# One found order for every instruction of a delta-rule and mixture-of-experts kernel

## The chip, the cores and the metric

The kernel runs on one core of one Trainium2 chip. Its time is the device time of one launch in microseconds (us).

## The reference, cut to what matters

Three stages, float32 throughout. An attention layer keeps a 48x48 state for each of 32 heads and updates it token by token over 768 tokens (the delta rule). Its output, 3072 rows of 384, is routed: each row goes to one of 8 experts, a two-layer network of its own. The result goes through a last network with three first matrices, of whose outputs the largest is taken.

```python
for t in range(S):                                  # S = 768, for 4 x 8 heads, D = 48
    y[:, :, t] = einsum('bhd,bhde->bhe', q[:, :, t], state)
    v_old = einsum('bhde,bhd->bhe', state, k_n[:, :, t])
    state = state + beta[t] * einsum('bhd,bhe->bhde', k_n[:, :, t], v[:, :, t] - v_old)
logits = x @ w_gate + modality_bias[modality_id]    # x: 3072 x 384; 8 experts
e_idx = argmax(logits); gate_w = softmax(logits)[e_idx]
out[e_idx == e] = gate_w * (relu(x @ w1[e]) @ w2[e])   # 384 -> 1024 -> 384, for each e
h = maximum(maximum(x2 @ m1, x2 @ m2), x2 @ m3)        # 384 -> 768
return h @ m_out                                       # 768 -> 384
```

## The kernel before, in words

**Attention.** The 768 tokens are cut into 12 chunks C of 64; two chunks make a group g of 128. Every matrix is split into a high and a low 16-bit half, and a product is three matmuls (`mm3`, L145 to L147). For a group, `k_load`, `k_norm` and `k_split` load, scale and split the keys. For a chunk, `st_G` makes the products of the keys among themselves, and `g_out` and `at_load` carry them through DRAM into a layout in which `sub` inverts a triangular 32x32 system for all heads: 31 steps, each with a product (`stmp`, L508) and a difference (`W`, L510) on VectorE, and from step 10 on also on GpSimd. The inverse goes to DRAM (`Wd`) and back (`w_load` to tile `N`, then `w_split`). `st_Z`, `st_X`, `st_P` prepare the chunk; `st_R`, `st_U`, `st_S`, `st_O` are the recurrence. `st_S` of chunk C makes the state that chunk C+1 needs, `st_O` the output rows. "o" is the half of the heads; `st_S.4.0` is that step for chunk 4, half 0.

**Routing.** `route0` and `route1` of a chunk make logits, the expert of each row and its slot, and scatter the rows to the DRAM buffer `xs` (L745), where each expert has its own stretch. `select` picks the expert that has most rows waiting; after the last chunk `pad_zero` copies eight blocks of zero rows behind the experts' rows (L785).

**Experts.** `tiles` works through 12 tiles of 256 rows (one of 288). For a tile `tile_load` reads the expert's number and first row into registers (L800, L801) and loads the rows transposed (`mxT`, L804). The weights come in 8 parts f (`ws`, L817, L819, two buffers), are split on ScalarE and GpSimd (`wh` L827, `wl` L139), and used by `up` (`hp`, L838) and `down` (`accA`, `accB`, L867). The last network of the tile before (`second`: `pa`, `pb`, L888; `outp`: `po`, L905) goes between them. The step `more` advances this generator by half a part. `narrow_load` and `narrow` bring the last network's weights in and split them.

**What sets the order.** `STEPS` lists every step. Those ahead of a bar are given out as they stand, each engine runs them in that order. Those behind it carry a number after "@", which sets a priority, and a list scheduler orders the single instructions of all engines at build time by priority and by a timeline of its own. `side()` gives some instructions a higher priority there. What follows `STEPS` in `run` (the last tiles) goes through the same scheduler. Every engine then runs its own list in order, and so does each queue that issues loads and stores, SyncE's (SP) above all. The loop at the end of `run` runs over the rows that are left, here none.

Of the kernel before, what the change touches and what calls it, by code (L numbers as in the profile page):

```python
# [1 line left out]

# [6 lines left out]
F16 = mybir.dt.float16  # L9
# [10 lines left out]
WIDE = 288  # L20
RS = 3072 + WIDE
ZROW = 8 * RS
XROWS = ZROW + WIDE
XW = 784
MAGIC = 12582912.0
STEPS = """
# [89 lines left out]


AHEAD = 20000
class Kern:
    def __init__(self, tc, ctx, q, k, v, beta, mod_id, w_gate, mod_bias, w1, w2, m1, m2, m3, m_out, out):  # L120
        self.tc, self.nc, self.ctx = tc, tc.nc, ctx
# [5 lines left out]
        self.w1, self.w2, self.m, self.m_out, self.out = w1, w2, (m1, m2, m3), m_out, out  # L127
        self.S = q.shape[2]
        self.NG = self.S // 128
        self.NT = 4 * self.NG  # L130
        self.NC = 2 * self.NG

    def pool(self, ctx, name, bufs, **kw):
        return ctx.enter_context(self.tc.tile_pool(name=name, bufs=bufs, **kw))

    def lo(self, eng, out, in_, hi, scale=1.0):
        nc = self.nc
# [12 lines left out]
    def setup(self):  # L150
        nc, NG, ctx = self.nc, self.NG, self.ctx
        P = lambda n, b, **kw: self.pool(ctx, n, b, **kw)
        self.dr1 = P("dr1", 1, space=DRAM)
        self.dr = P("dr", 3, space=DRAM)
        self.c0 = P("c0", 1)
        self.tp = self.tile_pools(ctx, "a", 2, 3, False)
        self.sel = P("sel", 1)
        P = lambda n, b, **kw: self.pool(self.actx, n, b, **kw)
        self.psC = P("psC", 2, space=PSUM)
        self.psZ = P("psZ", 1, space=PSUM)  # L160
        c1 = self.c1 = P("c1", 1)
        self.ld = P("ld", 1)
        self.mg = P("mg", 1)
        self.ch = P("ch", 2)
        self.rt = P("rt", 1)
        self.xs = self.dr1.tile([XROWS, XW // 2], I32, name="xs")
# [535 lines left out]
    def route(self, C):  # L702
        nc, rt, x = self.nc, self.rt, [self.x[C, o] for o in range(2)]
# [14 lines left out]
        m2 = rt.tile([128, 2, 1], F32, name="m2")  # L718
# [23 lines left out]
        slot = rt.tile([128, 2], I32, name="slot")  # L742
        V.tensor_copy(slot, sl)
        for o in range(2):
            nc.gpsimd.indirect_dma_start(  # L745
                out=self.xs[:, :], out_offset=bass.IndirectOffsetOnAxis(ap=slot[:, o:o + 1], axis=0),
                in_=x[o][:, :], in_offset=None)
        yield

# [32 lines left out]
        return ri  # L782

    def pad_rows(self, r):
        self.nc.sync.dma_start(out=self.xs[bass.ds(r, WIDE), :], in_=self.xs[ZROW:XROWS, :])  # L785

    def pad_zero(self):
        nc, mx = self.nc, self.sel
# [7 lines left out]
    def tile_load(self, si, tp=None):  # L796
        nc = self.nc
        tp = tp or self.tp
        mx, w = tp["x"], tp["W"]
        e = nc.sync.value_load(si[0:1, 0:1], min_val=0, max_val=7)  # L800
        row = nc.sync.value_load(si[0:1, 1:2], min_val=0, max_val=ZROW)  # L801
        T = dict(e=e, w=w, tp=tp, ws={}, wb={}, cols=[(t, min(128, w - t)) for t in range(0, w, 128)])
        T["xT"] = mx.tile([128, 6, w], F16, name="mxT", bufs=3)
        nc.sync.dma_start_transpose(out=T["xT"], in_=self.xs[bass.ds(row, w), 0:384].bitcast(F16))  # L804
        T["ix"] = mx.tile([128, len(T["cols"]), 2], I32, name="ix", bufs=3)
        full = w // 128
        nc.sync.dma_start(out=T["ix"][:, 0:full], in_=self.xs[bass.ds(row, 128 * full), 384:386].rearrange("(t p) w -> p t w", p=128))
        if w > 128 * full:
            nc.sync.dma_start(out=T["ix"][0:w - 128 * full, full], in_=self.xs[bass.ds(row + 128 * full, w - 128 * full), 384:386])
        self.wt_load(T, 0)  # L810
        self.wt_load(T, 1)
        return T

    def wt_load(self, T, f):
        nc, e = self.nc, T["e"]
        ws = T["tp"]["w"].tile([128, 2, 384], F32, name="ws")
        nc.sync.dma_start(out=ws[:, 0].rearrange("p (k f) -> p k f", f=128),  # L817
                          in_=self.w1[bass.ds(e, 1), :, f * 128:(f + 1) * 128].rearrange("o (k p) f -> p (o k) f", p=128))
        nc.sync.dma_start(out=ws[:, 1], in_=self.w2[bass.ds(e, 1), f * 128:(f + 1) * 128, :].rearrange("o p d -> p (o d)"))  # L819
        T["ws"][f] = ws  # L820

    def wt_cast(self, T, f):
# [75 lines left out]
    def outp(self, T, t):  # L898
        nc, H = self.nc, T["H"]
        at, n = T["cols"][t]  # L900
        po = T["tp"]["psM"].tile([128, 384], F32, name="po", tag="m")
        i = 0
        for f in range(6):
            for a, b in (("h", "h"), ("h", "l"), ("l", "h")):
                nc.tensor.matmul(po[0:n], lhsT=H[a][:, f, at:at + n], rhs=self.mo[b][:, f], start=(i == 0), stop=(i == 17))  # L905
                i += 1
        ob = T["tp"]["x"].tile([128, 384], F32, name="ob", bufs=2)
        with self.side():
            nc.scalar.activation(ob[0:n], po[0:n], AF.Copy, scale=T["ix"].bitcast(F32)[0:n, t, 1:2])
        nc.gpsimd.indirect_dma_start(  # L910
            out=self.out[:, :], out_offset=bass.IndirectOffsetOnAxis(ap=T["ix"][0:n, t, 0:1], axis=0), in_=ob[0:n], in_offset=None,
            bounds_check=self.NT * 128 - 1, oob_is_err=False)

    def behind(self, T, f):
# [49 lines left out]
        next(self.moe)  # L964

    def side(self):
        return self.tc.high_priority(offset=AHEAD)

    def play(self, steps):
        tc = self.tc  # L970
        for step in steps.split():
            step, at = step.split("@")
            name, *args = step.split(".")
            tc.cur_priority = int(at) * 1000 + 1000000
            getattr(self, name)(*(int(a) if a.isdigit() else a for a in args))

    def run(self):
        nc, tc = self.nc, self.tc
        self.actx = ExitStack()
        self.setup()  # L980
        self.pieces, self.narrows, self.sis, self.moe = self.second_weights(), [], [], None
        E = mybir.EngineType
# [6 lines left out]
        self.sis.append((self.select(True),))  # L989
        for _ in self.moe:  # L990
            pass
        ri = self.remaining()
        regs = nc.values_load(ri[0:1, 0:1], min_val=0, max_val=18)
        with tc.For_i(0, regs, 1):
            for _ in self.tiles([(self.select(True),)]):
                pass
# [38 lines left out]
```

## Time and profile before

| | us |
|---|---|
| median of 3 runs | 973.54 |
| lowest, highest | 968.46, 976.4 |
| the profiled execution | 976.38 |
| its span, first to last instruction | 974.7 |

The profile is of one execution; 1.7 us of its time lie outside the span, and it is 2.8 us above the median. Times in the rows below count from the span's start. A row of the windows view gives, for a stretch, its length and then the busy time of each engine with the number of its instructions, TensorE's granted clock as a share of 2.4 GHz, and the share and rate of the DMA engines. In a row of a timeline or of the chain the first number is the start and the second the length.

### The profile page before, as it was taken

To read this page: it belongs to the slowest core of one execution; us is meant where nothing else is said; L and a number is where in the kernel's file an instruction comes from. 1 tells how busy PE (TensorE), PEld (TensorE's weight loads), DVE (VectorE), ACT (ScalarE), POOL (GpSimd) and SP (SyncE) were. 2 spreads that over 40 slices of the span, in tenths; PEclk is the share of its full clock that TensorE was granted. 3 is DMA by queue.
4 is the path that set the end of the run, shared out by engine and by line. 5 is a ranking of instruction groups with operands and counts; after the bars stand their busy time and mean duration, and the time that the engine had idled before them with its cause. 6 is when DMAs were issued, how large, how long until landed. Compare 5 with 4: busy or idle time off the path is not lost.

```text
span 974.7 us, 24604 instructions
## 1 busy us (share of the span) xinstructions
PE 701.5 (72%) x9442; PEld 580.6 (60%) x9442; DVE 646.8 (66%) x1552; ACT 434.8 (45%) x865; POOL 538.7 (55%) x694
## 2 busy tenths in 40 slices
PE   0324620487458877666788977899999997999994
PEld 0213520376337666565567756778788875887873
DVE  7688898688798499867998769757465441132220
ACT  2445542675344564434445534355364432344321
POOL 7173367556576677526767468664555443545421
PEclk9975855688568999879899989899999997999998
DMA  7796777786886737756688663456343345332200
GB/s 102 138 185 184 120 193 184 201 136 159 222 201 141 179 102 188 146 127 127 152 200 194 125 137 82 106 152 110 107 105 96 95 140 178 108 98 89 67 19 17
DMA packets 355322, 131.88 MB, mean 135 GB/s; under 512 B 290265, under 2 KB 346624, under 8 KB 355072
## 3 DMA queue, kind: packets, MB, share of 16 engines
q1 hardware_dynamic: 352096, 120.72, 54.5%
q0 software_dynamic: 3104, 9.54, 2.7%
q8 instruction: 76, 1.25, 0.5%
q14 instruction: 46, 0.38, 0.1%
HBM read 77.71 MB, written 34.10 MB: 115 GB/s over the span
## 4 chain that ended last, share of the span: by engine, by line
PE 29%; DVE 28%; DMA 7%; issue 6%; POOL 4%; ACT 3%; SPq 3%; POOLq 0%; DVEq 0%; ACTq 0%
PE pa L888 7%; DVE stmp L508 6%; PE hp L838 5%; DVE W L510 4%; PE pb L888 4%; PE po L905 4%; PE accA L867 3%; DMA xT<-xt 2%; PE accB L867 1%; DMA ws<-in_moe_w_dram 1%; DVE tl L581 1%; DMA xs<-xt,slot 1%; SPq L474 1%; POOL wl L139 1%; DVE hl L844 1%
## 5 line engine op out<-in xcount | busy, mean ns | idle before, releaser
L139 POOL TENSOR_TENSOR wl<-ws,wh 128x768 bf16<-128x768 f32 x96 | 159.2, 1659 | 71.3 <-ACT wh L827 69.4
L888 PE MATMUL pa<-x2T,mwh 128*128 128x256 f16 (+1 forms) x828 | 159.7, 284 | 14.7 <-DVE x2T L141 6.9
L838 PE MATMUL hp<-mxT,wh 128*128 128x256 f16 (+1 forms) x576 | 119.4, 283 | 49.1 <-ACT wh L827 42.3
L888 PEld LDWEIGHTS <-mwh 128*128 128x128 f16 x1296 | 129.8, 101 | 27.1 <-issue 7.6
L139 POOL TENSOR_TENSOR Hl<-mt,Hh 128x256 f16<-128x256 f32 (+1 forms) x72 | 49.8, 692 | 130.2 <-ACT Hh L895 127.9
L888 PE MATMUL pa<-x2T,mwl 128*128 128x256 f16 (+1 forms) x414 | 117.5, 284 | 0.0
L827 ACT ACTIVATE wh<-ws 128x768 f16<-128x768 f32 x96 | 80.5, 839 | 42.3 <-PE accB L867 21.5
L145 PEld LDWEIGHTS <-bkh 128*128 128x128 f16 x560 | 55.7, 106 | 59.8 <-DVE bkh L438 25.8
L508 DVE TENSOR_TENSOR stmp<-At,W 128x31 f32<-128x31 f32 (+29 forms) x155 | 88.2, 569 | 3.3 <-POOL At L497 0.4
L838 PEld LDWEIGHTS <-wh 128*128 128x128 f16 x576 | 57.7, 101 | 53.8 <-ACT wh L827 44.8
L888 PE MATMUL pb<-x2T,mwh 128*128 128x256 f16 (+1 forms) x432 | 86.7, 278 | 0.0
L844 DVE SCALAR_TENSOR_TENSOR hl<-hp,hh 128x256 f16<-128x256 f32 (+1 forms) x96 | 40.4, 421 | 66.5 <-ACT hh L843 62.9
L139 POOL TENSOR_TENSOR pl<-Pm,ph 64x512 f16<-64x512 f32 x48 | 57.0, 1188 | 47.6 <-ACT ph L634 39.1
L838 PE MATMUL hp<-mxT,wl 128*128 128x256 f16 (+1 forms) x288 | 81.4, 283 | 2.4 <-POOL wl L139 2.4
L895 ACT ACTIVATE Hh<-mt 128x256 f16<-128x256 f32 (+1 forms) x72 | 30.1, 418 | 104.6 <-DVE mt L894 104.5
L888 PEld LDWEIGHTS <-mwl 128*128 128x128 bf16 x648 | 65.1, 100 | 19.1 <-issue 9.5
L867 PEld LDWEIGHTS <-wh 128*128 128x128 f16 x576 | 57.6, 101 | 24.7 <-issue 15.6
L510 DVE TENSOR_TENSOR W<-W,stmp 128x31 f32<-128x31 f32 (+29 forms) x155 | 69.2, 447 | 3.0
L893 DVE TENSOR_TENSOR mt<-pa,mt 128x256 f32<-128x256 f32 x66 | 27.8, 421 | 61.1 <-ACT mt L892 57.5
L147 PEld LDWEIGHTS <-bkl 128*128 128x128 f16 x560 | 55.0, 106 | 8.3 <-issue 4.5
L888 PE MATMUL pb<-x2T,mwl 128*128 128x256 f16 (+1 forms) x216 | 59.9, 277 | 0.0
L867 PE MATMUL accA<-hh,wh 128*128 128x256 f16 (+1 forms) x184 | 52.0, 282 | 10.0 <-ACT hh L843 10.0
(286 smaller groups left out, 2583.6 us busy)
## 6 DMA issues: line engine op xcount, KB each, us to landing
ws<-in_moe_w_dram SPq DMA_DIRECT2D x192, 192.0 KB
nd<-in_moe_w_dram SPq DMA_DIRECT2D x18, 384.0 KB
vf<-in_v_dram SPq DMA_DIRECT2D x48, 96.0 KB
ring<-in_k_dram SPq DMA_DIRECT2D x10, 384.0 KB
ring<-in_q_dram SPq DMA_DIRECT2D x10, 384.0 KB
xs<-xs SPq DMA_DIRECT2D x8, 441.0 KB
N<-Wd SPq DMA_DIRECT2D x48, 64.0 KB
Qdh<-tmh SPq DMA_DIRECT2D x6, 512.0 KB
```

The costliest lines, as they stand in the source:

```text
L139: nc.gpsimd.tensor_tensor(out=out, in0=in_, in1=hi, op=ALU.subtract)
L145: mm(out, lhsT=ah, rhs=bh, start=start, stop=False)
L147: mm(out, lhsT=al, rhs=bh, start=False, stop=stop)
L508: E.tensor_tensor(out=tv, in0=At[:, j:j + 1, j + 1:].to_broadcast([128, m, n]), in1=W[:, r0:r1, j:j + 1].to_broadcast([128, m, n]), op=ALU ...
L510: E.tensor_tensor(out=W[:, r0:r1, j + 1:], in0=W[:, r0:r1, j + 1:], in1=tv, op=ALU.subtract)
L827: self.nc.scalar.activation(wh, ws, AF.Copy)
L838: nc.tensor.matmul(h, lhsT=a[:, 0, kk * 128:(kk + 1) * 128], rhs=xT[:, b], start=(n == 0), stop=(n == 8))
L844: nc.vector.scalar_tensor_tensor(out=hl, in0=h, scalar=0.0, in1=hh, op0=ALU.max, op1=ALU.subtract)
L867: nc.tensor.matmul(ps, lhsT=a[:, 1, ds], rhs=b, start=(f == 0 and i == 0 and d in first), stop=(f == 7 and i == 2 and d in last))
L888: nc.tensor.matmul(ps[i], lhsT=self.mw[a][:, i, kk, fs], rhs=x2T[:, b], start=(n == 0), stop=(n == 8))
L895: nc.scalar.activation(T["H"]["h"][:, f], mt, AF.Copy)
L905: nc.tensor.matmul(po[0:n], lhsT=H[a][:, f, at:at + n], rhs=self.mo[b][:, f], start=(i == 0), stop=(i == 17))
```

## The change

All calls that issue an instruction up to the last loop are recorded and not made. A `Book` stands in the place of `nc`: each call becomes an `Op`, and what it returns, a tile, a register or a pool, is a `Lazy` that is made when it is first asked for. Each instruction is a piece with a number of its own, in the order in which the source makes the calls; only matmuls that follow each other without a break share a piece, up to 32, or up to 9 in `more` and in the last tiles. `ORDER` is a list of all 4474 piece numbers. At the end the pieces are given out in that order, with no scheduler, for all five engines. The steps in `STEPS` and the instructions themselves stay as they were; the numbers after "@" and the bar are not used any more. Tiles take their buffers in the order of first use in `ORDER`. The loop behind stays as it was.

```diff
+ORDER = """
+2 6 3 0-1 180 5 23 13 179 181 8 63 12 14 178 148 19 9 4 21 7 66 11 22 83 105 10 84 20 17 15 18 106 16 150 29 146 85 80 149 77 43 86 55 74 81 31 36 70
...
+"""
+class Op(Lazy):
...
+    def get(self):
+        if not self.done:
+            self.done = True
+            self.val = self.fn(*real(self.args), **real(self.kw))
+        return self.val
...
+class Book:
...
+    def put(self, name, op):
+        if self.cut or name != "tensor" or self.pieces[-1][0] != name or len(self.pieces[-1][1]) == self.most:
+            self.pieces.append((name, []))
+            self.cut = False
+        self.pieces[-1][1].append(op)
...
+    def give(self, order):
+        assert sorted(order) == list(range(len(self.pieces))), (len(order), len(self.pieces))
+        for n in order:
+            for op in self.pieces[n][1]:
+                op.get()
+        self.open = False
...
     def side(self):
-        return self.tc.high_priority(offset=AHEAD)
+        return nullcontext() if self.nc.open else self.tc.high_priority(offset=AHEAD)
...
     def run(self):
-        nc, tc = self.nc, self.tc
+        tc, book = self.tc, self.nc
...
-        first, then = STEPS.split("|")
-        with tc.manual_schedule(engines={E.PE, E.DVE, E.Activation, E.Pool, E.SP}):
-            self.play(first)
-        self.play(then)
-        self.actx.close()
+        self.play(STEPS.replace("|", " "))
+        book.then(self.actx.close)
...
+        order = []
+        for run in ORDER.split():
+            a, _, b = run.partition("-")
+            order += range(int(a), int(b or a) + 1)
+        with tc.manual_schedule(engines={E.PE, E.DVE, E.Activation, E.Pool, E.SP}):
+            book.give(order)
         ri = self.remaining()
```

## Rows read from the trace of the kernel before

**Rows 1.** The page: busy time of each engine; the chain that ended last, by engine.

```profile
PE 701.5 (72%) x9442; PEld 580.6 (60%) x9442; DVE 646.8 (66%) x1552; ACT 434.8 (45%) x865; POOL 538.7 (55%) x694
...
PE 29%; DVE 28%; DMA 7%; issue 6%; POOL 4%; ACT 3%; SPq 3%; POOLq 0%; DVEq 0%; ACTq 0%
```

**Rows 2.** The windows view, by stage.

```profile
core 0: us, PE busy (x) PEld busy (x) DVE busy (x) ACT busy (x) POOL busy (x), PEclk, DMA share, GB/s
0.00:142.40 142.40, 46.47 (x960) 40.10 (x960) 116.38 (x264) 64.79 (x117) 69.79 (x163) 0.79 0.76 151
142.40:176.00 33.60, 0.00 (x0) 0.00 (x0) 25.05 (x66) 8.50 (x12) 21.93 (x35) 0.50 0.81 204
176.00:259.20 83.20, 51.41 (x1004) 42.75 (x1005) 66.37 (x145) 51.27 (x101) 47.22 (x42) 0.77 0.78 171
259.20:300.00 40.80, 25.45 (x181) 17.93 (x181) 39.12 (x87) 17.96 (x30) 29.67 (x31) 0.67 0.76 203
300.00:340.00 40.00, 35.61 (x380) 29.25 (x379) 21.83 (x52) 21.58 (x37) 27.53 (x40) 0.94 0.67 149
340.00:400.00 60.00, 47.23 (x697) 39.53 (x694) 57.20 (x123) 28.48 (x58) 45.16 (x65) 0.97 0.60 144
400.00:449.20 49.20, 34.17 (x619) 29.54 (x618) 31.30 (x89) 22.46 (x49) 21.10 (x23) 0.83 0.70 148
372.20:449.20 77.00, 54.87 (x971) 46.12 (x972) 58.18 (x152) 32.97 (x69) 39.55 (x55) 0.87 0.69 149
449.20:531.90 82.70, 64.79 (x894) 53.02 (x891) 78.01 (x170) 38.33 (x81) 60.56 (x79) 0.94 0.69 160
531.90:787.40 255.50, 229.45 (x3374) 194.78 (x3372) 168.74 (x445) 121.11 (x261) 142.79 (x158) 0.97 0.49 115
807.50:850.00 42.50, 35.46 (x284) 29.21 (x285) 7.55 (x19) 13.94 (x27) 18.59 (x16) 0.88 0.43 122
850.00:955.50 105.50, 105.14 (x877) 85.37 (x875) 25.14 (x57) 37.81 (x79) 42.09 (x38) 1.00 0.22 67
```

**Rows 3.** Timelines of TensorE, SP and VectorE around the first expert tile.

```profile
176.05 0.40 PE L838 MATMUL hp<-mxT,wh 128*128 128x256 f16 x1 [33.66 <-ACT wh L827]
...
157.16 7.00 SPq L325 DMA_DIRECT2D nd<-in_moe_w_dram  x3
167.70 1.48 SPq L804 DMA_TRANSPOSE mxT<-xs  x1
...
170.63 0.76 SPq L817 DMA_DIRECT2D ws<-in_moe_w_dram  x1
...
179.20 1.07 DVE L141 SCALAR_TENSOR_TENSOR ntl<-N,nth 128x512 f16<-128x512 f32 x1 [7.63 <-ACT nth L569]
```

**Rows 4.** Timelines of TensorE and GpSimd: the first matmuls of `st_G.7.0` and `st_S.4.0`, `at_load.3`.

```profile
321.89 0.19 PE L145 MATMUL G<-sth,bkh 128*128 128x64 f16 x1
...
372.16 0.32 PE L676 MATMUL S<-s0h,id 128*128 128x384 f16 x1
...
324.76 0.95 POOL L488 MEMSET W<- 128x1024 f32 x1 [1.51 <-DMA Wd<-W]
```

**Rows 5.** The page's costliest groups: the two VectorE lines of `sub`.

```profile
L508 DVE TENSOR_TENSOR stmp<-At,W 128x31 f32<-128x31 f32 (+29 forms) x155 | 88.2, 569 | 3.3 <-POOL At L497 0.4
...
L510 DVE TENSOR_TENSOR W<-W,stmp 128x31 f32<-128x31 f32 (+29 forms) x155 | 69.2, 447 | 3.0
```

**Rows 6.** The chain that ended last: from the last scatter to the end.

```profile
797.56 0.67 SPq L785
...
798.44 6.06 DMA xs<-xs
...
804.51 9.06 DMA ws<-in_moe_w_dram
...
814.94 3.84 PE pa L888 x18
...
950.08 1.98 PE pa L888 x18
```

More of the change, by code (lines that the diff above doesn't have):

```diff
@@ L1 @@
-from contextlib import ExitStack
+from contextlib import ExitStack, nullcontext
 import concourse.bass as bass
@@ new lines, with __init__, __getitem__, __call__ @@
+"""
+class Lazy:
+    def __init__(self, base, op=None):
+        self.base, self.op = base, op
+    def get(self):
+        if self.op is None:
+            return self.base
+        name, args, kw = self.op
+        b = self.base.get()
+        args, kw = real(args), real(kw)
+        if name == "[]":
+            return b[args[0]]
+        if name == "()":
+            return b(*args, **kw)
+        return getattr(b, name)(*args, **kw)
+    def __getitem__(self, i):
+        return Lazy(self, ("[]", (i,), {}))
+    def __call__(self, *args, **kw):
+        return Lazy(self, ("()", args, kw))
+    def __add__(self, n):
+        return Lazy(self, ("__add__", (n,), {}))
+    def rearrange(self, *args, **kw):
+        return Lazy(self, ("rearrange", args, kw))
+    def bitcast(self, *args):
+        return Lazy(self, ("bitcast", args, {}))
+    def to_broadcast(self, *args):
+        return Lazy(self, ("to_broadcast", args, {}))
@@ new lines, with __init__, get, tile @@
+class LazyTile(Lazy):
+    def __init__(self, pool, shape, dtype, kw):
+        self.pool, self.shape, self.dtype, self.kw, self.t = pool, shape, dtype, kw, None
+    def get(self):
+        if self.t is None:
+            self.t = self.pool.get().tile(self.shape, self.dtype, **self.kw)
+        return self.t
+class LazyPool:
+    def __init__(self, tc, ctx, kw):
+        self.tc, self.ctx, self.kw, self.p = tc, ctx, kw, None
+    def get(self):
+        if self.p is None:
+            self.p = self.ctx.enter_context(self.tc.tile_pool(**self.kw))
+        return self.p
+    def tile(self, shape, dtype, **kw):
+        return LazyTile(self, shape, dtype, kw)
@@ new lines, with __init__, get, real @@
+class Op(Lazy):
+    def __init__(self, fn, args, kw):
+        self.fn, self.args, self.kw, self.done, self.val = fn, args, kw, False, None
+    def get(self):
+        if not self.done:
+            self.done = True
+            self.val = self.fn(*real(self.args), **real(self.kw))
+        return self.val
+def real(x):
+    if isinstance(x, Lazy):
+        return x.get()
+    if isinstance(x, tuple):
+        return tuple(real(i) for i in x)
+    if isinstance(x, list):
+        return [real(i) for i in x]
+    if isinstance(x, dict):
+        return {k: real(i) for k, i in x.items()}
+    return x
@@ new lines, with __init__, __getattr__, put @@
+class Engine:
+    def __init__(self, book, name, eng):
+        self.book, self.name, self.eng = book, name, eng
+    def __getattr__(self, what):
+        fn = getattr(self.eng, what)
+        def put(*args, **kw):
+            op = Op(fn, args, kw)
+            if self.book.open:
+                self.book.put(self.name, op)
+            else:
+                op.get()
+            return op
+        return put
+class Book:
+    def __init__(self, nc):
+        self.nc, self.open, self.pieces, self.cut, self.most = nc, True, [], True, 32
+        for name in ("vector", "scalar", "gpsimd", "sync", "tensor"):
+            setattr(self, name, Engine(self, name, getattr(nc, name)))
+    def put(self, name, op):
[3 more added lines that the diff above has]
+        self.pieces[-1][1].append(op)
+    def step(self):
+        self.cut = True
+    def then(self, fn):
+        self.cut = True
+        self.put("none", Op(fn, (), {}))
+        self.cut = True
+    def give(self, order):
+        assert sorted(order) == list(range(len(self.pieces))), (len(order), len(self.pieces))
+        for n in order:
+            for op in self.pieces[n][1]:
+                op.get()
+        self.open = False
@@ L119 @@
 class Kern:
     def __init__(self, tc, ctx, q, k, v, beta, mod_id, w_gate, mod_bias, w1, w2, m1, m2, m3, m_out, out):
-        self.tc, self.nc, self.ctx = tc, tc.nc, ctx
+        self.tc, self.nc, self.ctx = tc, Book(tc.nc), ctx
         self.q = q.rearrange("b h s d -> (b h) s d")
@@ L126, in __init__ @@
         self.mod_id, self.w_gate, self.mod_bias = mod_id, w_gate, mod_bias
-        self.w1, self.w2, self.m, self.m_out, self.out = w1, w2, (m1, m2, m3), m_out, out
+        self.w1, self.w2, self.m, self.m_out, self.out = Lazy(w1), Lazy(w2), (m1, m2, m3), m_out, out
         self.S = q.shape[2]
@@ L165, in setup @@
         self.rt = P("rt", 1)
+        for p in (self.dr1, self.dr, self.c0, *(self.tp[k] for k in ("psA", "psM", "w", "x")), self.sel, self.psC, self.psZ, self.c1, self.ld, self.mg, self.ch, self.rt):
+            p.get()
         self.xs = self.dr1.tile([XROWS, XW // 2], I32, name="xs")
@@ L745, in route @@
             nc.gpsimd.indirect_dma_start(
-                out=self.xs[:, :], out_offset=bass.IndirectOffsetOnAxis(ap=slot[:, o:o + 1], axis=0),
+                out=self.xs[:, :], out_offset=Lazy(bass.IndirectOffsetOnAxis)(ap=slot[:, o:o + 1], axis=0),
                 in_=x[o][:, :], in_offset=None)
@@ L784, in pad_rows @@
     def pad_rows(self, r):
-        self.nc.sync.dma_start(out=self.xs[bass.ds(r, WIDE), :], in_=self.xs[ZROW:XROWS, :])
+        self.nc.sync.dma_start(out=self.xs[Lazy(bass.ds)(r, WIDE), :], in_=self.xs[ZROW:XROWS, :])
     def pad_zero(self):
@@ L803, in tile_load @@
         T["xT"] = mx.tile([128, 6, w], F16, name="mxT", bufs=3)
-        nc.sync.dma_start_transpose(out=T["xT"], in_=self.xs[bass.ds(row, w), 0:384].bitcast(F16))
+        nc.sync.dma_start_transpose(out=T["xT"], in_=self.xs[Lazy(bass.ds)(row, w), 0:384].bitcast(F16))
         T["ix"] = mx.tile([128, len(T["cols"]), 2], I32, name="ix", bufs=3)
         full = w // 128
-        nc.sync.dma_start(out=T["ix"][:, 0:full], in_=self.xs[bass.ds(row, 128 * full), 384:386].rearrange("(t p) w -> p t w", p=128))
+        nc.sync.dma_start(out=T["ix"][:, 0:full], in_=self.xs[Lazy(bass.ds)(row, 128 * full), 384:386].rearrange("(t p) w -> p t w", p=128))
         if w > 128 * full:
-            nc.sync.dma_start(out=T["ix"][0:w - 128 * full, full], in_=self.xs[bass.ds(row + 128 * full, w - 128 * full), 384:386])
+            nc.sync.dma_start(out=T["ix"][0:w - 128 * full, full], in_=self.xs[Lazy(bass.ds)(row + 128 * full, w - 128 * full), 384:386])
         self.wt_load(T, 0)
@@ L966, in side @@
     def side(self):
-        return self.tc.high_priority(offset=AHEAD)
+        return nullcontext() if self.nc.open else self.tc.high_priority(offset=AHEAD)
     def play(self, steps):
-        tc = self.tc
         for step in steps.split():
-            step, at = step.split("@")
+            step = step.split("@")[0]
             name, *args = step.split(".")
-            tc.cur_priority = int(at) * 1000 + 1000000
+            self.nc.step()
+            self.nc.most = 9 if name == "more" else 32
             getattr(self, name)(*(int(a) if a.isdigit() else a for a in args))
     def run(self):
-        nc, tc = self.nc, self.tc
+        tc, book = self.tc, self.nc
         self.actx = ExitStack()
```

91 lines of the change are left out of this document (84 added, 7 removed), and 66 rows, old and new, of the table ORDER.

## The prediction

> **What bounds the kernel now.** I read the page's busy times first: TensorE 702 us, VectorE 647, GpSimd 539, ScalarE 435 of a span of 974.7 [rows 1]. No engine fills the span, and the chain that ended last gives TensorE 29% and VectorE 28%: the bound changes from stage to stage. So I read the windows by stage [rows 2]. Up to 142 us VectorE is busy for 116 of 142 us: attention with no expert work to go beside it. From 142 to 176 TensorE does nothing. From 176 to 449 both engines are half full in turn: from 259 to 300 VectorE has 39.1 of 40.8 us and TensorE 25.5; from 300 to 340 TensorE has 35.6 of 40 and VectorE 21.8; from 340 to 400 VectorE has 57.2 of 60. From 449 to 532 VectorE is the fuller one (78.0 of 82.7). From 532 to 787 TensorE has 229.5 of 255.5, and behind 850 it is full (105.1 of 105.5). A new order changes no instruction. It can win only idle time of the engine that bounds a stage, and the clock of TensorE, granted at 0.67 to 0.83 where it idles much and at 0.94 to 1.00 where it does not [rows 2].
>
> **How I read the order.** Numbering the calls of the source as `Book` does gives 4474 pieces; looking up their places in `ORDER` gives each engine's list. I set it against the order in the trace, the same calls matched line by line. 117 of the 706 TensorE pieces and 63 of 1546 VectorE instructions keep their place; a VectorE instruction moves by 19 places on the mean. So the order is really another one, and the case that the change does nothing needs no chance of its own. From about 855 us on TensorE's list is nearly the same. One count carries most of what follows: how many of the 4122 expert matmuls stand ahead of an attention step on TensorE.
>
> | step (time before, us) | before | by the list |
> |---|---|---|
> | first expert tile done in part, `st_S.2.0` (199) | 63 | 45 |
> | `st_G.7.0` (322) | 441 | 225 |
> | `st_S.4.0` (372) | 720 | 414 |
> | last matmuls of `route1.5` (449) | 954 | 945 |
> | of `route1.6` (532) | 1341 | 1332 |
> | of `route1.9` (691) | 2169 | 2403 |
> | of `route1.11` (787) | 2772 | 2853 |
>
> Up to 260 us and at 449 to 532 both orders stand alike; between 260 and 449 attention is pulled ahead of expert work, behind 532 expert work ahead of attention. A matmul of 256 columns costs 0.109 us at full clock (18 in 1.98 us [rows 6]).
>
> **A, 142 to 180 us.** TensorE waits 33.7 us for the first expert weights [rows 3]. Behind the two register reads on SP came three loads of the last network's weights (157.2, 7.0 us) and the transposed rows `mxT`, issued at 167.7; only behind them, at 170.6, went the first `ws`. In the list the four `ws` come right behind the register reads, 13 us sooner. But `mxT` now stands behind them, behind four `v_load`, the store of `Wd`, the next two parts of `ws`, which must wait until GpSimd has freed a buffer, and the first load of `N`. `hp` needs `mxT` as well as `wh`. So of the 13 us little reaches TensorE; `N`, for which VectorE waits 7.6 us [rows 3], also comes sooner, by a few us. The gain is between 0 and 7.6; I take 3, nearer to the lower end because of what `mxT` is moved past.
>
> **B, 259 to 449 us.** VectorE idles 18.2 us from 300 to 340 and 17.9 from 400 to 449 [rows 2], 36 in all, and in the stretches beside them it is full. The first hole is there because `at_load.3`, which starts the next inversion, comes at 324.8, behind `st_G.7`, whose first matmul came at 321.9 [rows 4], and TensorE had done 441 expert matmuls by then. The list has 216 fewer ahead, 23.5 us at full clock, so the 31 steps of `sub.3` can begin in the hole. VectorE's list agrees: 67 instructions go from ahead of the last one of `st_S.4.1` to behind it and none the other way, 31.4 us by their own durations, of which 33 belong to `sub` (group means of 0.57 and 0.45 us [rows 5], 15.3 us by their own) and 20 to the expert stage. Nothing is removed: at `route1.5` VectorE has done 402.1 us of work by the list against 400.5. So the gain is the idle time that is filled and no more, 0 to 36 us. Filling asks that the expert matmuls which are put off find room later: 306 of them (33 us) between `st_S.4.0` and `route1.5`, and TensorE idled 22.1 us from 372 to 449 [rows 2]. I take 20: most of the first hole (14), for which the list has a visible cause, and a third of the second (6), for which I see none. What is late next is TensorE.
>
> **C, 449 to 787 us.** From 449 to 532 VectorE has 4.7 us left, so I count nothing there. From 532 to 787 TensorE idles 26 us [rows 2]. By the list it has up to 234 more expert matmuls to do ahead of a routing, and at the last one 81 more, 8.8 us. Where they fall into idle time the tail is shorter by so much; where they push the routing back nothing is won. Bounds 0 and 8.8; I take 4. SP is in order: the two transposed loads of chunk 11 now stand behind two pairs of `ws` more, which wait for buffers. That costs nothing as long as the last tile's rows are there in time. By the list the 288-row tile starts 414 matmuls (45 us) behind the last routing, against 486 (53 us) before, and its rows wait for the zero copies, which had landed 17 us behind the last routing, at 804.5 [rows 6].
>
> **D, 787 to 850 us.** The eight copies of zero rows (first issued at 797.6) stood together on SP ahead of the next weights; their data took until 804.5, the weights issued then took 9.1 us more, and TensorE stood from 807.5 to 814.5 [rows 6]. It came back slow, 18 matmuls in 3.84 us against 1.98. From 807.5 to 850 it idled 7.0 us and its clock was 0.88 [rows 2]; 12% of 35.5 busy us is 4.3. Together 11.3 us. In the list these weights stand ahead of the last routing's register reads, and the eight copies lie singly between later weights. I take 9 of 0 to 11.3: the cause is gone, but some later `ws` still shares the DMA engines with 441 KB copies.
>
> **What costs nothing.** The two stretches ahead of 142 us: TensorE is idle for most of it and VectorE's list has 132.9 us of work up to the end of `route1.1` against 136.1, a difference inside A. Small shifts of `xt<-tok`, `memset` and `q_spread` fill VectorE's or GpSimd's idle time. Behind 855 us the lists agree; TensorE is full there and I change nothing.
>
> **Sum.** 3 + 20 + 4 + 9 = 36 us off the profiled execution's 976.4, so 940.4; that execution is 2.8 us above the median of 973.5, so 937.5 for the median.
>
> **The rivals.** *The engines trade waits* (0.21): B and C give nothing, since each hole that is filled opens another beside it, with A and D as above: 12 us, so 961.5. For it speaks that VectorE is full around both holes and that the second has many small waits; against it that the first has one cause which the list removes.
>
> *TensorE is thinned out and falls behind* (0.13): `st_S.4.0` comes no sooner than 372, because VectorE is already full from 259 to 300 and from 340 to 400. Then the 306 matmuls put off, 33.3 us, are owed in a stretch of 77 us in which TensorE was busy for 54.9: 11 us late at `route1.5` at the clock of 0.87. Where TensorE idled more the clock was 0.67 and 0.77 [rows 2]; at 0.72 the busy time is 66.3 and the debt 46.3, 36 us late. The middle is 23, less A and D: 11 us slower, 984.5. It decides from `st_S.4.0` on: if that comes ahead of about 360 the debt is covered.
>
> By the Trainium skill (TensorE: Matmul & The Clock Gate, HAM oscillation) idle gaps of TensorE put its clock back to the low level, and matmuls should be grouped so that no wait falls between the groups; by it expert work should not be spread thin as this order does from 260 to 450, and this second rival would be what comes. The trace agrees on the clock: 0.67 where TensorE was busy for 25.5 of 40.8 us, 0.94 where it was for 35.6 of 40 [rows 2]. By that rule alone B would be a loss. I hold against it that VectorE and not TensorE ends the waits there.
>
> **How the numbers follow.** The forecast, 937.5 us, has a chance of 0.66, with 912 to 955 as its own range: B and C at their upper ends and A and D as taken give 917, and a little of A and D more makes 912; B at a quarter of what I took gives 952. With 0.21 for 961.5 and 0.13 for 984.5, the range that leaves out no more than 2 in 10 is 906 to 978. The low end is every term at its upper bound: 7.6 + 36 + 8.8 + 11.3 = 64 us off 973.5 is 910, and some clock that TensorE wins back where it is fuller, a few us. A measurement of this kernel can tell a change from none from about 1%, 964 to 983. Faster than that: the forecast and half of the first rival, 0.76. Within: the other half, and a small part of the second, 0.13. Slower: 0.11.
>
> **What would show it.** A: TensorE's wait ahead of the first `hp` shorter than 33.7 us by a few, `N` in use ahead of 178. B: `st_G.7.0` near 300 and `st_S.4.0` ahead of 360, VectorE over 85% busy from 300 to 450, `route1.5` near 430. C: the last routing near 760 with TensorE over 92% busy ahead of it. D: no stop of 7 us behind the last routing and a clock near 1.00. I am wrong if `st_S.4.0` comes at 372 or later, or if SP's queue holds back the transposed loads of the last chunks so that a tile starts late.

## The result, and the profile after

947.8 us at the median (945.57 to 951.75, 4 runs) against 973.6 (4 runs by then): a ratio of 0.9745 with a 95% interval of 0.9692 to 0.9798, some 25 us faster. The profiled execution took 948.81 us.

In the new kernel every instruction is given out at one source line, so all rows read L333. I told the steps apart by place: each engine runs its list in order, so the n-th instruction on an engine is the n-th of that engine in `ORDER`. First the page's busy times and the chain by engine, as in [rows 1].

```profile
PE 689.1 (73%) x9442; PEld 576.6 (61%) x9442; DVE 625.1 (66%) x1552; ACT 437.1 (46%) x865; POOL 547.1 (58%) x694
...
PE 36%; DVE 7%; DMA 6%; issue 4%; SPq 3%; POOL 3%; ACT 2%; POOLq 0%; DVEq 0%; ACTq 0%
```

The same instructions, and VectorE's part of the chain is down from 28% to 7%. Next the windows of [rows 2] with the new kernel in them.

```profile
core 0: us, PE busy (x) PEld busy (x) DVE busy (x) ACT busy (x) POOL busy (x), PEclk, DMA share, GB/s
0.00:142.40 142.40, 36.62 (x832) 31.60 (x833) 95.74 (x216) 59.52 (x104) 78.35 (x184) 0.66 0.70 133
...
259.20:300.00 40.80, 20.67 (x191) 15.17 (x191) 37.51 (x91) 21.53 (x32) 32.14 (x38) 0.71 0.89 226
300.00:340.00 40.00, 20.39 (x228) 17.43 (x228) 29.32 (x68) 16.98 (x31) 30.03 (x45) 0.66 0.75 168
340.00:400.00 60.00, 50.66 (x686) 41.40 (x685) 52.21 (x113) 27.61 (x57) 43.63 (x57) 0.89 0.74 153
400.00:449.20 49.20, 45.18 (x705) 38.44 (x704) 36.56 (x97) 26.09 (x56) 28.21 (x29) 1.00 0.67 137
...
449.20:531.90 82.70, 74.68 (x1091) 64.20 (x1090) 73.84 (x200) 46.47 (x101) 64.08 (x80) 1.00 0.76 178
531.90:787.40 255.50, 238.69 (x3371) 202.42 (x3368) 177.09 (x457) 123.54 (x263) 150.71 (x163) 0.96 0.50 119
807.50:850.00 42.50, 42.50 (x363) 35.28 (x361) 10.40 (x24) 16.69 (x34) 19.72 (x17) 1.00 0.53 140
```

Up to 142 us VectorE did 20.6 us less work than before in the same time (95.7 against 116.4): the kernel starts worse. From 340 on TensorE is fuller in every stretch shown, and from 807 to 850 it doesn't stop. Three steps in TensorE's timeline answer to [rows 3, 4]: the first expert product, `st_G.7.0` and `st_S.4.0`.

```profile
186.35 0.37 PE L333 MATMUL hp<-mxT,wh 128*128 128x256 f16 x1 [26.22 <-DMA mxT<-xs]
...
302.77 0.24 PE L333 MATMUL G<-sth,bkh 128*128 128x64 f16 x1 [7.95 <-ACT bkh L333]
...
358.67 0.32 PE L333 MATMUL S<-s0h,id 128*128 128x384 f16 x1
```

The first comes 10.3 us later than before, the others 19.1 and 13.5 us sooner. So time is lost early and more than that is won later; the loss stands in the timelines of VectorE, GpSimd, SyncE and TensorE in the opening. First the new kernel, then the same places in before.

```profile
52.86 0.20 DVE L333 TENSOR_SCALAR W<-bA 128x32 f32<-128x32 f32 x1 [14.97 <-POOL W L333]
...
51.88 0.95 POOL L333 MEMSET W<- 128x1024 f32 x1 [9.83 <-DMA Gx<-Gs]
...
44.26 1.24 SPq L333 DMA_TRANSPOSE sth<-mwh  x1
45.55 1.81 SPq L333 DMA_DIRECT2D nh<-Kdh  x2
47.40 0.66 SPq L333 DMA_DIRECT2D xs<-zero  x1
48.10 2.65 SPq L333 DMA_DIRECT2D Gx<-Gs  x4
50.79 0.62 SPq L333 DMA_DIRECT2D At<-Gd  x1
...
81.79 0.20 DVE L333 TENSOR_SCALAR mol<-bA 128x32 f32<-128x32 f32 x1 [9.86 <-POOL mol L333]
...
112.74 0.19 PE L333 MATMUL Z<-nnh,bgh 128*128 128x32 f16 x1 [27.23 <-DVE nnh L333]
```

```profile
35.55 2.65 SPq L478 DMA_DIRECT2D Gx<-Gs  x4
38.37 0.49 SPq L487 DMA_DIRECT2D At<-Gd  x1
...
40.07 0.95 POOL L488 MEMSET W<- 128x1024 f32 x1 [20.45 <-DMA Gx<-Gs]
...
42.73 1.23 DVE L497 TENSOR_TENSOR At<-At,bA 128x1024 f32<-128x1024 f32 x1 [3.81 <-DMA At<-Gd]
```

The four `Gx<-Gs` go out at 48.1 behind transfers of a later use (before: 35.6). GpSimd's clear of `W`, which takes the buffer of `Gs`, waits for them; VectorE waits 15.0 us for the clear (before: 3.8 us for `At`), and the load of `At` leaves at 50.8 (before: 38.4). At 81.8 the first instruction of `sub.1` has held VectorE for 9.9 us in the middle of `sub.0`. `sub.0` ends at 102 us instead of 71, TensorE waits 27.2 us for what follows from it, and `st_S.0.0` comes at 121.9 instead of 94.8.

### The profile page after: what moved, and what is told of

Same layout as the page of the kernel before. It is cut to its first block, busy times and chain, and to the rows that moved or that the text cites. A ratio compares the mean times of both kernels' runs of the same rounds, so it can differ in the third digit from the quotient of the medians.

```text
span 947.1 us, 24591 instructions
## 1 busy us (share of the span) xinstructions
PE 689.1 (73%) x9442; PEld 576.6 (61%) x9442; DVE 625.1 (66%) x1552; ACT 437.1 (46%) x865; POOL 547.1 (58%) x694
## 4 chain that ended last, share of the span: by engine, by line
PE 36%; DVE 7%; DMA 6%; issue 4%; SPq 3%; POOL 3%; ACT 2%; POOLq 0%; DVEq 0%; ACTq 0%
PE pa L333 9%; PE hp L333 6%; PE pb L333 5%; PE po L333 4%; PE accA L333 3%; SPq L333 3%; PE accB L333 2%; DMA ws<-in_moe_w_dram 2%; PE R L333 1%; DVE stmp L333 1%; DMA xs<-xt,slot 1%; POOL wl L333 1%; DMA out_dram<-ob,ix 1%; DMA xT<-xt 1%; PE O L333 1%
## 5 line engine op out<-in xcount | busy, mean ns | idle before, releaser
L333 POOL TENSOR_TENSOR wl<-ws,wh 128x768 bf16<-128x768 f32 x96 | 161.4, 1685 | 94.9 <-ACT wh L333 84.0
L333 PE MATMUL pa<-x2T,mwh 128*128 128x256 f16 (+1 forms) x828 | 163.5, 283 | 11.2 <-DVE mt L333 5.6
L333 PEld LDWEIGHTS <-wh 128*128 128x128 f16 x1152 | 115.3, 100 | 53.0 <-ACT wh L333 18.1
L333 PEld LDWEIGHTS <-mwh 128*128 128x128 f16 x1296 | 131.5, 101 | 24.0 <-DVE mt L333 2.5
L333 PE MATMUL hp<-mxT,wh 128*128 128x256 f16 (+1 forms) x576 | 116.2, 281 | 29.0 <-DMA mxT<-xs 26.7
L333 PE MATMUL pa<-x2T,mwl 128*128 128x256 f16 (+1 forms) x414 | 117.1, 283 | 0.0
L333 PEld LDWEIGHTS <-bkh 128*128 128x128 f16 x1120 | 63.0, 106 | 73.8 <-ACT bkh L333 38.5
L333 ACT ACTIVATE wh<-ws 128x768 f16<-128x768 f32 x96 | 80.8, 842 | 58.6 <-PE accB L333 34.5
L333 POOL TENSOR_TENSOR Hl<-mt,Hh 128x256 f16<-128x256 f32 (+1 forms) x72 | 52.3, 726 | 70.8 <-ACT Hh L333 65.2
L333 DVE SCALAR_TENSOR_TENSOR hl<-hp,hh 128x256 f16<-128x256 f32 (+1 forms) x96 | 40.2, 420 | 78.1 <-ACT hh L333 77.2
L333 PE MATMUL hp<-mxT,wl 128*128 128x256 f16 (+1 forms) x288 | 81.3, 282 | 11.5 <-POOL wl L333 11.5
L333 PE MATMUL pb<-x2T,mwh 128*128 128x256 f16 (+1 forms) x432 | 89.4, 287 | 0.0
L333 DVE TENSOR_TENSOR stmp<-At,W 128x31 f32<-128x31 f32 (+29 forms) x155 | 80.8, 521 | 6.1 <-POOL At L333 4.3
L333 PEld LDWEIGHTS <-wl 128*128 128x128 bf16 x576 | 57.5, 100 | 35.1 <-POOL wl L333 13.1
L333 PEld LDWEIGHTS <-mwl 128*128 128x128 bf16 x648 | 65.7, 101 | 20.1 <-issue 10.1
L333 DVE TENSOR_TENSOR W<-W,stmp 128x31 f32<-128x31 f32 (+29 forms) x155 | 67.9, 438 | 1.9
L333 POOL TENSOR_TENSOR pl<-Pm,ph 64x512 f16<-64x512 f32 x48 | 58.0, 1208 | 17.8 <-ACT ph L333 15.6
L333 PE MATMUL accA<-hl,wh 128*128 128x256 f16 (+1 forms) x184 | 51.4, 279 | 15.0 <-DVE hl L333 14.2
L333 PE MATMUL pb<-x2T,mwl 128*128 128x256 f16 (+1 forms) x216 | 62.1, 287 | 0.0
L333 PEld LDWEIGHTS <-bkl 128*128 128x128 f16 x560 | 54.4, 106 | 10.9 <-issue 9.6
L333 ACT ACTIVATE hh<-hp 128x256 f16<-128x256 f32 (+1 forms) x96 | 36.7, 382 | 49.6 <-PE hp L333 45.4
L333 ACT ACTIVATE Hh<-mt 128x256 f16<-128x256 f32 (+1 forms) x72 | 30.0, 416 | 62.8 <-DVE mt L333 62.5
```

The lines of the kernel that those rows point to most:

```text
L333: self.val = self.fn(*real(self.args), **real(self.kw))
```

## The experiments

Pieces can be put in any order that keeps what each reads and writes in sequence, so an experiment is another list. The list of before is read from its trace: the pieces in the order in which they started.

**Control, and the worth of each stretch.** The recording with before's own list; then lists that follow before for the pieces that had started by a time T there, and the found order for all others. The seam for T = 449, as an example:

```diff
 ORDER = """
-2 6 3 0-1 180 5 23 13 179 181 8 63 12 14 178 148 19 9 4 21 7 66 11 22 83 105 10 84 20 17 15 18 106 16 150 29 146 85 80
+2-3 0 5 1 4 6 10 13 7 11 8 14 12 83 15 9 16-19 84 23 85 24 86 25 20-21 26 87 22 27 77 28 78 29 79 30 80 31-36
...
+2167 2209 2267 2168 2149 2199 2150 2350 2201 2204 2241 2205 2242-2243 2206 2351
...
```

The fourth number there, 2168, is the last that had started by 449 us.

> The order in which the kernel before's pieces were started on the chip, read from its trace, written down as the list of the kernel after: the same pieces through the same recording, none of the found order. Theory (the found order alone makes the gain): 968 to 979 us, ratio to before 0.995 to 1.005, span of the profiled run near 975. Rival (the recording itself, which puts the program together in another way, makes part of it): clearly below 965 us.

> Pieces that the kernel before had started by 787 us in its order, the tail alone in the found order. Theory (D: the 7 us stop behind the last routing and the starved matmuls behind it go): 962 to 968 us, ratio 0.987 to 0.993. Rival (in before's state at 787 us the tail has as little ready as before, so the found order can't fill it): 971 to 976 us. The distance to the run that changes over at 449 us is the worth of the stretch 449 to 787: 4 us by the prediction, some 20 to 28 by the trace of after.

> Pieces that the kernel before had started by 449 us in its order, all others in the found order. By the prediction's terms only C and D are left: 13 us below before, 956 to 965 us. By the trace of after the gain lies behind 449 us: 30 to 37 us below before, 935 to 946 us. The distance to the run that changes over at 259 us is the worth of the found order between 259 and 449 us: 20 us by the prediction, 0 to 5 by the trace of after.

> Pieces that the kernel before had started by 259 us in its order, all others in the found order. As the prediction's terms have it (B 20 us between 259 and 449, C 4, D 9): 33 us below before, 937 to 945 us. As the trace of after reads (B near nothing, some 37 us won between 449 and 700, some 10 lost between 700 and 784, D 6 to 10): also some 30 to 37 us below before, 935 to 945 us; this run is the upper step of a ladder and tells by its distance to the next one.

> The pieces that the kernel before had started by 150 us, in its order, and then all others in the found order. Theory (the found order loses its 18 to 27 us in the opening for good): sub.0 done near 71 us instead of 102, st_S.0.0 near 95 us instead of 122, first product of an expert (hp) at or below 176 us, and 923 to 938 us in all, ratio to before 0.95 to 0.965. Rival (the opening's lag is taken up by a later wait that the transfer of mxT sets): within 4 us of after, 944 to 952 us.

| before's list up to | median, us | ratio to before, 95% | step, us |
|---|---|---|---|
| the end (control) | 974.4 | 0.9977 (0.9950 to 1.0004) | |
| 787 | 966.1 | 0.9936 (0.9908 to 0.9965) | -4.0 |
| 449 | 944.6 | 0.9716 (0.9662 to 0.9770) | -21.4 |
| 259 | 939.2 | 0.9663 (0.9625 to 0.9701) | -5.2 |
| 150 | 934.3 | 0.9576 (0.9532 to 0.9619) | -8.5 |
| 0 (after) | 947.8 | 0.9745 (0.9692 to 0.9798) | +16.5 |

A step is the difference of two ratios times 973.6; by the two intervals it is good to 4 to 7 us, so the 5.2 us from 259 to 449 can't be told from nothing. (Each ratio is against runs of before made beside that list; by the medians alone the opening's step is 13.5 us.) A step also holds what its own seam costs, of which more under D below. The control's interval holds 1, and its 974.4 us lie where its theory put them: the recording makes none of the gain. The found order is worth 21 us between 449 and 787, little in the stretches beside that, 8.5 between 150 and 259, and it loses 16.5 us ahead of 150. At 449 the prediction's terms had 956 to 965 us and the reading of the new kernel's trace 935 to 946; 944.6 came. The list with before's opening beats both kernels: 0.9576, 16.5 us better than the change itself.

**The found opening by itself.** The pieces of T = 150 in the found order among themselves, then before's rest.

```diff
 ORDER = """
 2 6 3 0-1 180 5 23 13 179 181 8 63 12 14 178 148 19 9 4 21 7 66 11 22 83 105 10 84 20 17 15 18 106 16 150 29 1
...
-754 1496 755 758-759 762 1083 938 669 900 1084-1086
+1494 1497 1495-1496 938 664-665 680 666 683 798
...
```

> The same pieces (those that the kernel before had started by 150 us), but in the found order among themselves, and then all others in the order of before. Theory (the opening costs by itself and the rest of before passes it on): 985 to 1000 us, ratio 1.01 to 1.03, with st_S.0.0 near 120 us. Rival (slack of the rest takes it up): 970 to 980 us, ratio 0.995 to 1.007.

991.3 us, 1.0158 (1.0107 to 1.0209), `st_S.0.0` at 121.4: against the control 17.6 us slower. Two ways to the same loss, 16.5 and 17.6 us. Of the 27 us by which `st_S.0.0` is late, some 17 reach the end.

**Mending the opening piece by piece.** Two moves first: on SyncE `g_out.1.d` (141 to 144), `g_out.0.x` and `.1.x` (153 to 156) and the load of `At` (167) go ahead of `n_load.0` (223 to 226), `k_turn.2` (169, 170) and `zero_rows` (184); and the 107 pieces of `sub.0` (in 239 to 363) ahead of `sub.1`.

```diff
-124 151 225 140 163 226 160 141 353 162 142 354 170 355 144 356 143 357 169 358 223-224 184 153 155-156 206 154 205 167
+124 151 140 163 141 142 144 143 167 155 156 153 154 225 226 160 353 162 354 170 355-357 169 358 223-224 184 206 205
```

> The found order with two groups of pieces moved: the transfers g_out.1.d, g_out.0.x, g_out.1.x and at_load.0 ahead of n_load.0, k_turn.2 and zero_rows in SyncE's queue, and all of sub.0 ahead of the first piece of sub.1's load and clear. Theory (these two places make the opening's loss): VectorE's idle times of 15.0 us at 38 to 53 and of 9.9 us at 72 to 82 are gone or under 4 us each, st_S.0.0 at 95 to 103 us instead of 122, and 925 to 938 us in all. Rival (other pieces of the opening hold it back, or the lag is taken up later anyway): st_S.0.0 above 112 us, or 943 us and more.

942.8 us, 0.9636 (0.9585 to 0.9687), yet `st_S.0.0` only at 119.2: the rival was right that other pieces hold it back. VectorE still stood for 10.0 us at 38 and 14.5 at 72. GpSimd's timeline says why, and VectorE's beside it:

```profile
64.44 1.42 POOL L333 TENSOR_TENSOR bg2l<-Go,bg2h 32x256 f16<-32x256 f32 x2 [16.41 <-ACT bg2h L333]
65.93 1.40 POOL L333 TENSOR_TENSOR bgl<-Go,bgh 32x256 f16<-32x256 f32 x2
67.29 0.21 POOL L333 TENSOR_TENSOR stmp<-At,W 128x21 f32<-128x21 f32 x1
...
64.33 0.26 DVE L333 TENSOR_TENSOR W<-W,stmp 128x100 f32<-128x100 f32 x1
64.63 0.60 DVE L333 TENSOR_TENSOR stmp<-At,W 128x90 f32<-128x90 f32 x1
65.26 0.70 DVE L333 TENSOR_TENSOR W<-W,stmp 128x90 f32<-128x90 f32 x1
...
67.46 0.23 DVE L333 TENSOR_TENSOR stmp<-At,W 128x70 f32<-128x70 f32 x1
```

`g_split.0` stood at the head of GpSimd's list and waited 16.4 us for ScalarE's half of that step, which needs a transfer (`Go`); GpSimd's whole part of `sub.0`, which needed nothing more, stood behind it and ended at 85. So the next list keeps the first move and puts VectorE's and GpSimd's part of `sub.0` ahead of `g_split.0` and of `sub.1`, the clear for `sub.2` (1065) and its first operation (1140) behind `sub.1`, and `Wd` (363) with `w_load.0` (396 to 399) directly behind the load for `sub.1` (359):

```diff
-615 277 620 311 359 618 278 312 281 360
+617 615 620 359 363 398 397 396 399 618 360
...
-370 659 371 398 1065 372 397 660 396 1140 373 399
+1236 1065 1140 1139 1119
```

> The found order with the first of the two moves of before (SyncE's transfers) and three more: GpSimd's and VectorE's part of sub.0 ahead of g_split.0 (for which GpSimd sat idle from 48.0 to 64.4 us in the run with two moves) and of sub.1, the clear for sub.2 and its first operation behind sub.1, and the writing of Wd and w_load.0 directly behind at_load.1. Theory (pieces that wait at the head of GpSimd's, VectorE's and SyncE's lists make the opening's loss): sub.0 done on GpSimd near 67 us instead of 85, st_S.0.0 at 97 to 110 us instead of 119, and 930 to 939 us. Rival (the transfers' own time in the opening holds it): st_S.0.0 still above 114 us, 941 to 948 us.

939.5 us, 0.9685 (0.9626 to 0.9744); `sub.0` done on GpSimd at 67, but `st_S.0.0` at 115.7, on the rival's side of 114, while the time is just over the theory's range. SyncE's timeline:

```profile
79.52 1.37 SPq L333 DMA_TRANSPOSE stl<-tml  x1
80.99 1.17 SPq L333 DMA_DIRECT2D Qdh<-tmh  x1
82.26 0.37 SPq L333 DMA_DIRECT2D moh<-Gd  x1
82.68 0.82 SPq L333 DMA_DIRECT2D Wd<-W  x1
89.39 1.92 SPq L333 DMA_DIRECT2D N<-Wd  x4
```

`Wd` was ready at 67 and left at 82.7, behind loads and stores of the next chunks. I moved 24 pieces of those behind `w_load.1`:

```diff
-418 428 729 414 439 732 423 419 415 417
+418 428 407 406 434 436-437 435 490-491 614 617 615 620 618 616 619 432 621 433 492 561 560 493 563 562 729 414 439 732 423
```

> The mended opening of the run before (found_opening_mended), and 24 pieces more moved: the transfers that the first chunk doesn't need yet, with the splits that go with them (q_store.0 and .1, v_load.2, q_load.1, q_split.1, q_turn.1, q_spread.1, k_load.2), behind w_load.1. Theory (what is left of the opening's loss is SyncE's list: Wd was ready at 67 us and left at 82.7, N<-Wd was issued at 89 to 91 and landed at 103): Wd leaves by 76 us, w_split.0 starts by 92 us, st_S.0.0 at 98 to 106 us instead of 115.7, and 929 to 937 us. Rival (the postponed work, 2 MB of it, comes due later and takes back what it gave): st_S.0.0 as early, but 938 to 945 us.

943.2 us, 0.9717 (0.9683 to 0.9750). `Wd` left at 75.6 and `w_split.0` started at 88.4, as expected, and `st_S.0.0` came at 120.8, later than in either list before it. VectorE's timeline shows my own mistake:

```profile
91.09 0.39 DVE L333 TENSOR_TENSOR stmp<-moh,mol 128x192 f32<-128x192 f32 x1
107.45 1.11 DVE L333 COPY qh<-sth 64x1024 f16<-64x1024 f16 x2 [15.97 <-DMA sth<-Qdh]
```

`q_spread.1` had been moved to stand ahead of `w_spread.0` on VectorE, its data came 16.0 us later, and `w_spread.0`, long ready, stood behind it. One group on the wrong side of another took the gain away. The last list puts each group where its user stands:

```diff
-418 428 407 406 434 436-437 435 490-491 614 617 615 620 618 616 619 432 621 433 492 561 560 493 563 562 729 414 439 732 423
+418 428 407 406 432-434 436-437 435 729 414 439 732 423
...
```

> found_opening_mended once more, with the same late transfers moved back as in opening_transfers_late, but each group to where its own user stands: q_store.0, q_turn.1 and v_load.2 behind w_load.1, q_load.1, k_load.2, q_split.1 and q_store.1 behind n_load.1, and q_spread.1, on which VectorE stood 16.0 us in that run with w_spread.0 behind it, behind st_S.0. Theory (what is left of the opening's loss is pieces that wait at the head of a list): the stop of 16.0 us is gone, st_S.0.0 at 98 to 106 us, first product of an expert at 170 to 177 us, and 927 to 936 us, as good as b_open_then_found. Rival (the transfers themselves, whose order is now near before's, or GpSimd's share of sub.1): st_S.0.0 above 108 us, 937 to 944 us.

937.1 us, 0.9654 (0.9631 to 0.9677): `st_S.0.0` at 100.4 as the theory had it, but the first expert product at 178.3 and the time not in its range. `st_S.1.0` is still 15 us behind before: VectorE stands 8.5 us from 112.5 for `th`, and `n_load.1` leaves at 107 instead of 97. About 9 of the 16.5 us are mended, good to 6; the rest is not settled instruction by instruction.

By time alone the four mended lists can hardly be told apart: only the third and the last have intervals that don't overlap. And the time doesn't follow `st_S.0.0`: the last list has it 21.5 us sooner than the new kernel and is 9 us faster. What the time follows is the end of `route1.1` on VectorE: 165.8 us in the new kernel, 163.3, 159.6, 164.4 and 157.3 in the four lists and 152.0 with before's opening. In all six the first expert product comes 20.4 to 21.8 us behind it, and the medians stand in the same order (947.8; 942.8, 939.5, 943.2, 937.1; 934.3). This is read from the six traces; `route1.1` alone was not moved.

**Which engine's list carries the gain behind 449?** SyncE's found list with the others near before's (the first change below, against the list that changes over at 449), and the converse (the second); up to 449 us both are before's list.

```diff
-2209 2267 2168 2149 2199 2150 2350 2201 2204
+2209 2267 2168 2269 2215 2217 2257 2212 2280
...
-2210 2258 2280 2261 2281 2215 2217 2392
+2210 2258 2261 2215 2217 2392 2268 2269
...
```

> As b_449_then_found in SyncE's list only: behind 449 us SyncE follows the found order exactly, while the other engines keep before's order as nearly as SyncE's list lets them (a piece of TensorE stands 0.7 places from before's list on average, of VectorE 3.2). Theory (the gain behind 449 us comes from the compute engines' lists, which feed TensorE in the chain's gaps): 966 to 977 us. Rival (it comes from transfers that go out in a better order): 945 to 958 us.

> The converse: behind 449 us TensorE, VectorE, ScalarE and GpSimd follow the found order exactly, SyncE keeps before's order as nearly as these let it (a piece stands 1.5 places from before's list on average, 2.1 from the found one). Theory (compute lists): 942 to 952 us, as b_449_then_found. Rival (transfers): 957 us and more.

1127.2 us, 1.1590 (1.1527 to 1.1653), and 1104.0 us, 1.1379 (1.1332 to 1.1426). Neither expectation of the first came true; the second lies in its rival's open range (957 and more), but far above what that meant. SyncE's waits from 449 to 900 us in the first of them, what it waited for, the sum, the number and the longest:

```profile
SPq L330 <- POOL wl L330: 175.5, 26, 16.7
SPq L330 <- ACT tmh L330: 22.8, 2, 12.2
```

and in the list that changes over at 449 with all engines together, from 449 to 800:

```profile
SPq L332 <- POOL wl L332: 50.6, 22, 6.5
SPq L332 <- DVE ssel L332: 26.1, 4, 12.3
```

A `ws` load has to wait until GpSimd has freed its buffer. Where SyncE's list wants it sooner than GpSimd's list frees it, everything behind it on SyncE waits too: 175.5 us for this alone. In the second list SyncE waits longest for VectorE's `ssel` (53.3 us from 449 to 900), for `wl` 28.7. So the question can't be put this way: the lists of the found order fit each other and not before's, and in which of them the gain lies stays open. (Tiles take buffers by first use in the list, so these two also share buffers otherwise than either parent; how much of the 150 us that makes was not tried.)

## Why the prediction held, point by point

The sign and the range held: 947.8 lies in 906 to 978 and 10 us above 937.5. But that the sum came near is luck: 36 us were forecast in four terms, the ladder has 39 us behind 150, most of them in other stretches than forecast, and a loss of 16.5 ahead of it that was put at nothing.

**What costs nothing: the step that failed first.** "The two stretches ahead of 142 us" cost 16.5 us. I compared how much VectorE work stands ahead of `route1.1` (132.9 against 136.1 us) and took the order within it for harmless because TensorE is idle there. The sum of work says nothing about who waits: VectorE's idle time up to 142 us went from 26.0 to 46.7 us [rows 2], and the mended lists show that pieces at the head of SyncE's, GpSimd's and VectorE's lists make about 9 us of the loss.

**A (3 us): nothing.** The wait ahead of the first `hp` fell from 33.7 [rows 3] to 26.2 us and is now ended by `mxT`, as the step said. With before's opening the first product comes at 173.8 us against 175.5 in the control, but that trace is 2.9 us ahead already at `st_S.0.0` (91.8 against 94.7), up to which the two lists agree; other lists that agree up to the first product have it at 172.8 to 176.8. So nothing of A is to be seen, its lower bound; in the new kernel `N` is in use at 188.7, not ahead of 178. The step from 150 to 259 is worth 8.5 all the same: what of it shows in the traces lies behind 176 us, where I had costed nothing.

**B (20 us): too large.** `st_G.7.0` at 302.8 and `st_S.4.0` at 358.7 came where the prediction said (before has only the first matmul of `st_S.4.0` at 372.2 and the last at 382.7, with others between; the new kernel has them together). But from 259 to 449 VectorE was busy for 155.6 of 190 us against 149.5 [rows 2], 82% and not over 85%: 6.1 us of 36 filled. The hole at 300 shrank from 18.2 to 10.7 us and that at 400 from 17.9 to 12.6, while 340 to 400, full before, got 7.8 us of its own. That is the first rival's mechanism; `route1.5` came at 457.9 and not near 430. The new kernel enters this stretch late, so two lists that agree up to 259 show it better. The one that changes over at 259, then the one at 449:

```profile
259.20:449.20 190.00, 139.38 (x1881) 115.84 (x1882) 148.80 (x351) 90.85 (x171) 126.26 (x162) 0.87 0.72 161
...
259.20:449.20 190.00, 141.50 (x1839) 115.44 (x1838) 149.27 (x347) 89.25 (x170) 121.30 (x156) 0.86 0.68 157
```

Here `st_G.7.0` also comes 24 us sooner (297.0 against 321.0), but VectorE does no more work, and `route1.5` comes at 451.5 against 452.7: no hole is filled on balance, and the ladder's 5.2 us are within its noise.

**C (4 us): too small, and the step that failed was the sentence that VectorE, with 4.7 us left from 449 to 532, leaves nothing to win.** The stretch to 787 is worth 21.4 us. The windows of the control:

```profile
449.00:532.00 83.00, 65.95 (x888) 54.47 (x887) 78.26 (x171) 38.29 (x80) 60.04 (x77) 0.89 0.69 156
532.00:640.00 108.00, 88.87 (x1307) 74.81 (x1304) 84.73 (x225) 46.74 (x102) 65.98 (x87) 0.94 0.54 124
```

and of the list that changes over at 449:

```profile
449.00:532.00 83.00, 72.98 (x1037) 61.70 (x1035) 75.44 (x188) 44.73 (x96) 64.57 (x80) 0.95 0.73 169
532.00:640.00 108.00, 100.56 (x1442) 86.52 (x1443) 90.93 (x207) 53.12 (x111) 73.78 (x88) 0.97 0.57 133
```

VectorE is as full as before, and TensorE gets 18.7 us more done by 640. Up to the last matmul of `route1.6` (536.4 and 522.5 us) VectorE was busy for 81.8 us in the control and 66.1 in this list; by the instructions' own durations, which overlap, 9.7 us of the difference are in `sub.4`, whose result isn't due yet; it is caught up by 640, where VectorE has room (90.9 against 84.7 us). The last routing comes at 778.2 against 790.3, with 90 more expert matmuls done ahead of it, 9.8 us at full clock: 21.9 in all, which agrees with the ladder; in the new kernel it comes at 782.3, not near 760. A full engine isn't a bound when part of what fills it can wait. That the putting off is the cause is read from the two traces; moving `sub.4` alone was not tried, and whether the order of the transfers has a part in it the two mixed lists couldn't tell.

**D (9 us).** The stop went and the clock from 807 to 850 is 1.00, as said: the only wait of TensorE that the waits view names from 780 to 850 is

```profile
PE pa L333 <- ACT mt L333: 2.3, 1, 2.3
```

against 7.1 us of before in front of `hp`. By the ladder the tail alone is worth 4.0 us (0 to 8), 5 less than I took. But part of what it wins pays for the seam: with before's list up to 787 TensorE has 126 expert matmuls to do between the first and the second part of the last routing, 36 in the control and 27 in the found order. The second part comes 9.1 us later; the control, then that list:

```profile
790.05 0.17 PE L331 MATMUL rkp<-oh,upper 128*128 128x16 f16 x1
...
799.13 0.17 PE L332 MATMUL rkp<-oh,upper 128*128 128x16 f16 x1
```

From the last routing to the end that list takes 164.0 us and the control 183.3. The 90 matmuls that are done by then account for 9.8 of the difference; the other 9.5 are near the 9 I took. Between 4.0 and 9.5 D isn't settled.

**The second rival** didn't come. The Trainium skill (TensorE: Matmul & The Clock Gate, HAM oscillation) advises to do all the matmuls of a tile ahead of a wait for data, so that TensorE keeps its clock. The trace agrees on the clock: 0.66 from 300 to 340, where TensorE was busy for 20.4 of 40 us, against 0.94 at 35.6 [rows 2]. But `st_S.4.0` was early, and from 340 to 449 TensorE did 95.8 us of work against 81.4: the debt was paid at a clock of 0.89 and 1.00. The rival's price had a slip: the 33.3 us of its first sum are at full clock, at 0.87 they are 38.3 and the lag 16 us and not 11, so its middle was some 3 us too low; its chance doesn't hang on that.

## What to carry to other kernels

When an order changes, don't ask how much work stands ahead of a step, ask what stands at the head of each engine's list while it waits, SyncE's first: a piece that is placed 10 us too soon blocks all that is ready behind it. An engine that is full in a stretch is a bound only if all of what it does there is due; look for what could wait (C, read from two traces and not tested by itself). And a found order is to be judged by stretch, with lists that change over at several times, and with an eye on what each seam costs: here its opening lost 16.5 us of some 40, and a list with the old opening and the new rest beat both.

## What the runs showed of the hardware

In the run with two moves VectorE's difference on 128x100 elements took 0.26 us, begun while GpSimd idled, the smaller ones on 128x90 0.60 and 0.70 us while GpSimd ran `g_split.0`, and the one on 128x70 0.23 us when that was over (rows above). The Trainium skill (SBUF — State Buffer, "SBUF: two separate sides") says that an operation of VectorE with two inputs in SBUF and one of GpSimd that reads SBUF exclude each other; these rows agree, with a factor of 2.3 to 2.7 on 128x90 even against the larger 128x100. VectorE's busy time isn't a measure of its work: with the same instructions it was 625.1 us in the new kernel and 642.2 in the faster one with before's opening. How much of that difference is this exclusion wasn't worked out.
